# Weight pieces one a block, from one queue, in a sliding-window attention kernel with a two-token expert

## The chip, the cores and the metric

The kernel runs on one core of one Trainium2 chip. The metric is the device time of that core in microseconds; the kernel before takes 795.97 (median of three runs, 795.15 to 799.0). A difference under about half a per cent is not told from no change.

## The reference

One sequence of 2048 tokens, width 640, bf16. Two branches share the normalised input `xn`:

```
xn = layernorm(x)
s  = attention(xn):  q = xn @ wq, 32 heads of width 192;  keys and values are the last 512 rows
                     of the caches;  softmax(q k^T / sqrt(192)) v;  all heads @ wo
B  : r = xn @ w_r;  the 2 tokens with the largest r go through
       y = (silu(x_sel @ w_gate) * (x_sel @ w_up)) @ w_down * sigmoid(r_sel)   (inner width 1536)
     B = xn, with y added at those two rows
out = x + s * silu(B)
```

Nearly all the arithmetic is the attention. The expert touches two rows, but its three weights (640 x 1536, twice, and 1536 x 640) must be loaded whole.

## The kernel before

**Blocks.** The heads are taken in 8 groups of 4. A step is one group's pair of heads for 512 tokens; it has two blocks, each with two score tiles (halves `a` = 0 and 1) of 128 tokens by 2 heads by 512 keys. There are 128 blocks; a round of 16 belongs to one group. The first 12 and the last 2 have an order written out by hand (`FIRST`, `LAST`); blocks 12 to 125 all run

`BLOCK = "A S0 M0 W m E0 B S1 M1 P E1 l"`

- `A`, `B` (`q_phase`, L340): the two halves of the query product for the next step; ScalarE then copies the result out (L352).
- `S0`, `S1` (L367): score products. `M0`, `M1` (L372): row maxima on VectorE. `E0`, `E1` (`exps`, L377): the exponentials on ScalarE, then at once the transpose `pT` of that half by a DMA from SP (L381). The exponentials' buffer `p_ring` has two blocks, so `E0` of block b waits until the transpose of block b - 2 has landed.
- `P` (`o_item` of block b - 2): products with the values (L406), between the two halves whatever stands in `bg[b]`; then scaling on ScalarE and VectorE and the transpose `oT` from SP (L423).
- `W` (`w_item` of block b - 6, L447): product with `wo`, added into `s_acc` by VectorE.
- `m` runs what stands in `mid[b]`, `l` what stands in `end[b]` and `loads[b]`.

**The next group's data.** `group_loads` puts keys, query weights, values and output weights of the next group at fixed blocks of each round, all on SP's queue. GpSimd reorders keys (`k_order`, L121) ahead of their DMA transpose from SP (L125), and copies output weights to the other half of the partitions (`wo_double`, L151).

**The second branch** is spread over blocks 11 to 105 by the lists `bg`, `mid`, `end` and `loads`; nothing else sets its place. All instructions are written in one order and each engine takes its own in that order. Blocks 12 to 28 compute r, 28 to 41 find the two tokens and normalise them into `xsT`. Then:

- `m_ffn_piece(fb, q, eng)` (L751): one of ten pieces (128 partitions x 512, 128 KB) of third `fb` of gate and up, into one buffer `wgu`. That buffer and `wd`, `y4` and `y_bc` are one place in memory: each waits until the one ahead is used up.
- `m_ffn(fb)`: `mul` (products L787, in `bg`; the copy and the tanh), `act` on GpSimd, `turn` (the transpose `hT` from SP, L802).
- `m_wd_piece(h, q)` (L809): one of six pieces (160 KB) of half `h` of the down weight, always from ScalarE. `m_down(h)` (L827): its product. `m_sig` scales the selection masks.
- `m_sum`, `m_own_gate`, `m_change`: the two result rows are summed, gated, and the change in them written to memory and broadcast to all partitions (`y_bc`, 640 KB) from GpSimd's queue.
- `m_gate(n)`: silu of token tile n in place in `xn`: a tanh on ScalarE (L863), two products on GpSimd. `m_add(n)` (L877, L878): adds the two changed rows by mask, on GpSimd.
- `fin_load(n)`: token tile n of x on SP. `fin_pre(n)` (L941, L942): GpSimd multiplies `s_acc` by the gate and adds x. The last group's `w_item` then only adds its own part.

ScalarE's and SP's transfers are issued in each engine's own program order, so whatever a transfer waits for holds up the instructions behind it on that engine.

Of the kernel before, what the change touches and what calls it, by code (L numbers as in the profile page):

```python
# [21 lines left out]
def kernel(ctx, tc, A_x, A_k_cache, A_v_cache, A_wq, A_wo, B_x, B_w_r, B_w_gate, B_w_up, B_w_down, out):  # L22
    nc = tc.nc
# [10 lines left out]
    DC = D // P  # L34
    FC = F // P
# [38 lines left out]
    def f_tile(shape, dtype, name, kind="q"):  # L74
        return banks[kind].tile(shape, dtype, name=name, tag="f")
# [405 lines left out]
    bg = defaultdict(list)  # L481
    mid = defaultdict(list)
    end = defaultdict(list)
    loads = defaultdict(list)
# [260 lines left out]
    def m_ffn_piece(fb, q, eng):  # L745
        def f():
            if q == 0:
                M["wgu"] = M["w"].tile([P, 2, DC, 512], BF16, name="wgu", tag="w")
            w, dc = divmod(q, DC)
            src = (B_w_gate, B_w_up)[w].rearrange("(c p) f -> p c f", p=P)  # L750
            eng.dma_start(out=M["wgu"][:, w, dc, :], in_=src[:, dc, fb * 512:(fb + 1) * 512])  # L751
        return f
# [28 lines left out]
    def m_ffn(fb):  # L781

        def mul():
            gu = f_tile([P, 2, P], FP32, "gu_ps")
            for dc in range(DC):
                for c in range(4):
                    nc.tensor.matmul(gu[32 * c:32 * c + 32], lhsT=M["xsT"][:, dc, :], rhs=M["wgu"][:, :, dc, c * P:(c + 1) * P],  # L787
                                     start=(dc == 0), stop=(dc == DC - 1), skip_group_check=True)
            th = M["s"].tile([P, 3, P], FP32, name="th", tag="t2")
            nc.vector.tensor_copy(out=th[:, 0:2], in_=gu)  # L790
            nc.scalar.activation(out=th[:, 2], in_=th[:, 0], func=ACT.Tanh, scale=0.5)
            M["th"] = th

        def act():
            th = M["th"]
            M["h"] = M["s"].tile([P, P], BF16, name="h")
            nc.gpsimd.tensor_tensor(out=th[:, 2], in0=th[:, 2], in1=th[:, 0], op=ALU.mult)
            nc.gpsimd.tensor_tensor(out=th[:, 2], in0=th[:, 2], in1=th[:, 0], op=ALU.add)
            nc.gpsimd.tensor_tensor(out=M["h"], in0=th[:, 2], in1=th[:, 1], op=ALU.mult)

        def turn():
            nc.sync.dma_start_transpose(out=M["hT"][:, fb * 4:(fb + 1) * 4, :].rearrange("p c t -> p (c t)"), in_=M["h"])  # L802
        return mul, act, turn

    def m_wd_piece(h, q):
        def f():
            if q == 0:
                M["wd"] = M["w"].tile([P, FC, HD], BF16, name="wd", tag="w")
            nc.scalar.dma_start(out=M["wd"][:, 2 * q:2 * q + 2, :],  # L809
                              in_=B_w_down.rearrange("(c p) d -> p c d", p=P)[:, 2 * q:2 * q + 2, h * HD:(h + 1) * HD])  # L810
        return f
# [10 lines left out]
    def m_down(h):  # L822
        def f():
            ys = f_tile([P, HD], FP32, "y_ps")
            for fb in range(FB):
                for c in range(4):
                    nc.tensor.matmul(ys[32 * c:32 * c + 32], lhsT=M["hT"][:, fb * 4 + c, :], rhs=M["wd"][:, fb * 4 + c, :],  # L827
                                     start=(fb == 0), stop=(fb == FB - 1), skip_group_check=True)
            if h == 0:
                M["yp"] = M["s"].tile([P, D], FP32, name="yp", tag="t2")  # L830
                nc.vector.tensor_scalar(out=M["yp"][:, 0:HD], in0=ys, scalar1=M["wrow"][:, 0:1], scalar2=None, op0=ALU.mult)
            else:
                nc.scalar.activation(out=M["yp"][:, HD:D], in_=ys, func=ACT.Copy, scale=M["wrow"][:, 0:1])
        return f
# [32 lines left out]
    def m_gate(n):  # L867
        def f():
            tz = M["s"].tile([P, D], FP32, name="tz", tag="t2")
            gate_of(tz, xn[:, n, :], xn[:, n, :])  # L870
        return f

    def m_add(n):
        def f():
            for j in range(2):
                yh = M["s"].tile([P, D], FP32, name="yh", tag="t2")
                nc.gpsimd.tensor_scalar(out=yh, in0=M["y_bc"][:, j, :], scalar1=M["oh"][:, n, j:j + 1], scalar2=None, op0=ALU.mult)  # L877
                nc.gpsimd.tensor_tensor(out=xn[:, n, :], in0=xn[:, n, :], in1=yh, op=ALU.add)  # L878
        return f
# [16 lines left out]
        if it is not None:  # L896
            spot(29 + b).append(it)
    loads[41].append(m_xsT)
    pieces = {0: (33, (2, 2, 2, 1, 2, 1)), 1: (43, (2, 2, 2, 2, 2)), 2: (49, (2, 2, 2, 1, 2, 1))}
    for fb, km in enumerate((43, 49, 57)):  # L900
        k0, counts = pieces[fb]
        q = 0
        for b, n in enumerate(counts, k0):
            loads[b].append(m_ffn_piece(fb, q, nc.scalar))
            if n == 2:
                mid[b + 1].append(m_ffn_piece(fb, q + 1, nc.sync))
            q += n
        mul, act, turn = m_ffn(fb)
        bg[km].append(mul)
        mid[km + 1].append(act)  # L910
        loads[km + 1].append(turn)
    for h in range(2):
        for q, a in enumerate((57, 58, 58, 59, 59, 60)):
            loads[a + 6 * h].append(m_wd_piece(h, q))
    mid[60].append(m_sig)
    bg[62].append(m_down(0))
    bg[69].append(m_down(1))
    bg[70].append(m_sum)
    for n, b in enumerate((28, 29, 45, 46, 47, 48, 51, 52, 53, 54, 55, 56, 59, 60, 61, 71)):
        bg[b].append(m_gate(n))  # L920
        bg[75 + 2 * n].append(m_add(n))
    bg[27].append(lambda: nc.scalar.preload_act_table_set("exp_and_others"))
    bg[72].append(m_own_gate)
    bg[73].append(m_change)


    def fin_open():
# [5 lines left out]
    def fin_load(n):  # L933
        def f():
            fin_x[n] = fin_pool["x"].tile([P, D], BF16, name="x_fin")
            nc.sync.dma_start(out=fin_x[n], in_=x_v[:, n, :])
        return f

    def fin_pre(n):
        def f():  # L940
            nc.gpsimd.tensor_tensor(out=s_acc[:, n, :], in0=s_acc[:, n, :], in1=xn[:, n, :], op=ALU.mult)  # L941
            nc.gpsimd.tensor_tensor(out=s_acc[:, n, :], in0=s_acc[:, n, :], in1=fin_x[n], op=ALU.add)  # L942
        return f

    bg[106].append(fin_open)
    for n in range(NTB):
        loads[108 + n].append(fin_load(n))
        bg[110 + n].append(fin_pre(n))

    LAG = 6  # L950
    BLOCK = "A S0 M0 W m E0 B S1 M1 P E1 l".split()
# [89 lines left out]
```

## Time and profile before

| | |
|---|---|
| median of the runs | 795.97 us |
| the profiled execution | 797.2 us, of which the span from first to last instruction is 795.3 |
| TensorE clock granted | 0.998 |
| busy: TensorE, VectorE, ScalarE, GpSimd | 776.7, 580.2, 527.6, 338.8 us |
| transfers of gate and up: ScalarE's queue, SP's queue | 17, 13 (128 KB each) |
| transfers of down: ScalarE's queue | 12 (160 KB each) |
| transposes pT, oT on SP's queue by DMA | 246, 126 |

In the profile PE is TensorE, DVE VectorE, ACT ScalarE, POOL GpSimd; a q behind an engine's name is its queue, where transfers are issued and which does no arithmetic. A row of the timeline has start and length in us, the line of the kernel, what is written from what, and how often; in brackets the engine's idle time ahead of it and what seems to have ended that. The chain is followed back from the last instruction: at each step to what let it start. In it a DMA row runs from issue to landing.

### The profile page before, as it was taken

The numbers are of one execution on the slowest core, as the hardware profiler recorded it, in microseconds if no ns is written. First come the engines' busy times: TensorE is split into PE (matmuls) and PEld (weight loads), VectorE is DVE, ScalarE is ACT, GpSimd is POOL, SyncE is SP. The second block draws the span as 40 slices with busy tenths as digits, with TensorE's granted clock in tenths as the row PEclk, the third lists the DMA queues.
The fourth block names the chain that finished last, engine by engine and source line by source line (L and its number), as shares of the span: only waits on it lengthen the run. The fifth ranks groups of instructions, "written<-read, shape, count | busy, mean of one in ns | idle before, by whom it ended". The sixth has DMA issues, their size and how long they took to land.

```text
span 795.3 us, 26980 instructions
## 1 busy us (share of the span) xinstructions
PE 776.7 (98%) x11356; PEld 572.9 (72%) x11356; DVE 580.2 (73%) x1069; ACT 527.6 (66%) x954; POOL 338.8 (43%) x280
## 2 busy tenths in 40 slices
PE   8899999999999998999999999999999999999997
PEld 4457677777777775777677777777777777777775
DVE  7898788887787775767666666767777767766775
ACT  6676666677666675776666766666666666666662
POOL 1333120023210234344311569847954741555875
PEclk9999999999999999999999999999999999999999
DMA  9989999999999999999999999999999999999992
GB/s 236 196 170 173 173 194 161 149 191 166 170 204 189 178 192 181 190 188 206 195 192 184 157 191 190 176 152 184 175 164 185 147 178 187 193 172 175 183 177 85
DMA packets 447130, 142.18 MB, mean 179 GB/s; under 512 B 414180, under 2 KB 446438, under 8 KB 447008
## 3 DMA queue, kind: packets, MB, share of 16 engines
q1 hardware_dynamic: 439184, 132.58, 99.3%
q10 hardware_dynamic: 6800, 5.02, 2.9%
q0 software_dynamic: 1024, 2.85, 1.3%
q8 instruction: 89, 1.46, 0.8%
q14 instruction: 33, 0.27, 0.1%
HBM read 40.31 MB, written 2.63 MB: 54 GB/s over the span
## 4 chain that ended last, share of the span: by engine, by line
PE 87%; DMA 5%; DVE 3%; ACT 3%; issue 1%; SPq 0%; ACTq 0%; DVEq 0%
PE w L447 24%; PE q_ps L340 23%; PE o_ps L406 20%; PE s L367 19%; DMA pT<-pexp 3%; ACT pexp L377 1%; DVE nm L372 1%; PE q_ps L309 1%; DMA oT<-o_sb 1%; DMA v_sb<-in_A_v_cache_dram 1%; DMA wgu<-in_B_w_up_dram 0%; ACT xnT L283 0%; DMA x_in<-in_A_x_dram 0%; PE tp L282 0%; SPq L381 0%
## 5 line engine op out<-in xcount | busy, mean ns | idle before, releaser
L372 DVE TENSOR_REDUCE nm<-s 128x2 f32<-128x1024 f32 x256 | 313.0, 1223 | 137.7 <-PE s L367 135.9
L377 ACT ACTIVATE pexp<-s,nm 128x512 bf16<-128x512 f32 x512 | 324.2, 688 | 98.3 <-DVE nm L372 89.1
L447 PE MATMUL w<-wo_g,oT 64*128 64x320 bf16 x3072 | 231.1, 296 | 1.6 <-DMA oT<-o_sb 1.6
L340 PE MATMUL q_ps<-xnT,wq_g 64*128 64x512 bf16 (+1 forms) x2340 | 232.6, 323 | 0.0
L367 PE MATMUL s<-kT,qT 64*128 64x512 bf16 x1536 | 211.6, 376 | 2.8 <-ACT pexp L377 2.5
L447 PEld LDWEIGHTS <-oT 64*128 64x128 bf16 x3072 | 170.1, 94 | 59.8 <-DMA oT<-o_sb 1.9
L406 PEld LDWEIGHTS <-pT 64*128 64x128 bf16 x4096 | 177.3, 94 | 31.0 <-issue 2.6
L406 PE MATMUL o_ps<-v_sb,pT 64*128 64x193 bf16 x4096 | 195.6, 243 | 2.2 <-DMA pT<-pexp 1.2
L420 ACT ACTIVATE o_sb<-o_ps,rl 128x192 bf16<-128x192 f32 x250 | 91.6, 418 | 131.7 <-DVE rl L413 126.5
L340 PEld LDWEIGHTS <-wq_g 64*128 64x128 bf16 x2340 | 125.8, 99 | 46.0 <-DVE qT L313 0.5
L367 PEld LDWEIGHTS <-qT 64*128 64x128 bf16 x1536 | 84.9, 94 | 57.8 <-issue 3.7
L151 POOL COPY wo_g<-wo_g 64x1920 bf16<-64x1920 bf16 x32 | 57.4, 1796 | 142.5 <-DMA wo_g<-in_A_wo_dram 133.9
L470 DVE TENSOR_TENSOR s_acc<-s_acc,w 128x320 f32<-128x320 f32 x192 | 85.0, 484 | 32.7 <-PE w L447 32.6
L352 ACT ACTIVATE qT<-q_ps 128x1024 bf16<-128x1024 f32 x114 | 92.4, 811 | 8.1 <-PE q_ps L340 2.1
L417 DVE TENSOR_TENSOR o_sb<-o_ps,rl 128x384 bf16<-128x384 f32 x131 | 73.0, 557 | 4.5
L121 POOL COPY k_perm<-k_raw 128x768 bf16<-128x768 bf16 x30 | 24.3, 824 | 104.7 <-DMA k_raw<-in_A_k_cache_dram 68.0
L877 POOL TENSOR_SCALAR yh<-y_bc,oh 128x640 f32<-128x640 f32 x32 | 60.2, 1882 | 6.1 <-DMA y_bc<-y_d 3.3
L864 POOL TENSOR_TENSOR tz<-tz,xn 128x640 f32<-128x640 f32 x16 | 22.4, 1398 | 65.2 <-ACT tz L863 65.2
L878 POOL TENSOR_TENSOR xn<-xn,yh 128x640 bf16<-128x640 bf16 x32 | 45.0, 1405 | 2.7
L413 DVE RECIPROCAL rl<-o_ps 128x2 f32<-128x2 f32 x256 | 30.6, 160 | 12.2 <-PE o_ps L406 7.7
L942 POOL TENSOR_TENSOR s_acc<-s_acc,x_fin 128x640 f32<-128x640 f32 x16 | 22.4, 1398 | 34.7 <-DMA x_fin<-in_A_x_dram 30.1
L478 POOL TENSOR_TENSOR fin_o<-fin_t,s_acc 128x640 bf16<-128x640 f32 x12 | 18.5, 1542 | 14.1 <-DVE fin_t L473 14.0
(138 smaller groups left out, 279.3 us busy)
## 6 DMA issues: line engine op xcount, KB each, us to landing
wo_g<-in_A_wo_dram SPq DMA_DIRECT2D x32, 240.0 KB, 4.1
k_raw<-in_A_k_cache_dram SPq DMA_DIRECT2D x32, 192.0 KB, 3.6
v_sb<-in_A_v_cache_dram SPq DMA_DIRECT2D x32, 192.0 KB, 4.3
wq_g<-in_A_wq_dram SPq DMA_DIRECT2D x14, 288.0 KB, 3.7
pT<-pexp SPq DMA_TRANSPOSE x246, 4.1
wq_g<-in_A_wq_dram SPq DMA_DIRECT2D x14, 192.0 KB, 3.9
x_fin<-in_A_x_dram SPq DMA_DIRECT2D x16, 160.0 KB, 3.5
oT<-o_sb SPq DMA_TRANSPOSE x126, 3.6
```

Of the source, the lines that this page charges most:

```text
L151: nc.gpsimd.tensor_copy(out=grp[g][("wo", pr)][half(1), cs, :], in_=grp[g][("wo", pr)][half(0), cs, :])
L340: mm = nc.tensor.matmul(q_ps[k][:, 0:n] if type(q_ps) is list else q_ps[:, k, 0:n], lhsT=wq[half(r), dc, c:2 * Dh:3], rhs=xnT[half(r), tok ...
L352: nc.scalar.activation(out=out, in_=q_ps[:, :, 0:n], func=ACT.Copy, scale=scale)
L367: nc.tensor.matmul(s_of[b, a][:, r, :], lhsT=qT_of[i][half(r), c, u * P:(u + 1) * P], rhs=grp[g][("kT", pr)][half(r), :, c, :], start=(c = ...
L372: rm = nc.vector.tensor_reduce(out=nm_of[b, a], in_=s_of[b, a], axis=AX.X, op=ALU.max, negate=True)
L377: nc.scalar.activation(out=p_ring[:, b % 2, a, :, hh, :].rearrange("p (x j) e -> p x j e", x=2), in_=s_of[b, a][:, hh, :].rearrange("p (j ...
L406: nc.tensor.matmul(o_of[b][r][:, a, 0:Dh + 1], lhsT=pT_ring[half(r), b % RP, a, k, :], rhs=v_ring[half(r), (g * PAIRS + pr) % RV, k, 0:Dh ...
L417: nc.vector.tensor_tensor(out=o_sb, in0=src, in1=rl[:, r].unsqueeze(2).unsqueeze(3).to_broadcast([P, 2, 3, HK]), op=ALU.mult)
L420: nc.scalar.activation(out=o_sb[:, a], in_=src[:, a], func=ACT.Copy, scale=rl[:, r, a:a + 1])
L447: nc.tensor.matmul(w_ps[r][:, 0:HD], lhsT=oT_ring[half(r), bs[pr] % RT, c, :], rhs=grp[g][("wo", pr)][half(r), c, cs], start=(pr == 0 and ...
L470: nc.vector.tensor_tensor(out=acc, in0=acc, in1=src, op=ALU.add)
L877: nc.gpsimd.tensor_scalar(out=yh, in0=M["y_bc"][:, j, :], scalar1=M["oh"][:, n, j:j + 1], scalar2=None, op0=ALU.mult)
```

## The change

All of it is in the lists of the second branch; no instruction is added or removed.

- Gate and up pieces: one a block, all from ScalarE, in blocks 32 to 41, 43 to 52 and 54 to 63. Before they were one or two a block in 33 to 38, 43 to 47 and 49 to 54; of two, the second was issued by SP in the next block's `m`, ahead of that block's transposes. That is 13 pieces that leave SP.
- Their products: 43, 54, 65 (before 43, 49, 57), with `act` and `turn` one block later as before.
- Down pieces: one a block in 65 to 70 and 72 to 77 (before 57 to 60 and 63 to 66, one or two a block). Their products: 72 and 79 (before 62, 69); the sum 80 (70); `m_own_gate` and `m_change` 82 and 83 (72, 73).
- Gates: 28, 29, 45 to 53, 56 to 60 (before 28, 29, 45 to 48, 51 to 56, 59 to 61, 71).
- Adds: sixteen from block 85 to 109, five in eight blocks (before every second block from 75 to 105).
- Last preparation: x loads from block 112 to 124, preparations 114 to 126, five in four blocks (before one a block from 108 and 110); the second branch's memory is given up in block 111 (before 106).

```diff
-    pieces = {0: (33, (2, 2, 2, 1, 2, 1)), 1: (43, (2, 2, 2, 2, 2)), 2: (49, (2, 2, 2, 1, 2, 1))}
-    for fb, km in enumerate((43, 49, 57)):
-        k0, counts = pieces[fb]
-        q = 0
-        for b, n in enumerate(counts, k0):
-            loads[b].append(m_ffn_piece(fb, q, nc.scalar))
-            if n == 2:
-                mid[b + 1].append(m_ffn_piece(fb, q + 1, nc.sync))
-            q += n
+
+    for fb, km in enumerate((43, 54, 65)):
+        for q in range(2 * DC):
+            loads[(32, 43, 54)[fb] + q].append(m_ffn_piece(fb, q, nc.scalar))
         mul, act, turn = m_ffn(fb)
         bg[km].append(mul)
         mid[km + 1].append(act)
         loads[km + 1].append(turn)
     for h in range(2):
-        for q, a in enumerate((57, 58, 58, 59, 59, 60)):
-            loads[a + 6 * h].append(m_wd_piece(h, q))
+        for q in range(FC // 2):
+            loads[65 + 7 * h + q].append(m_wd_piece(h, q))
     mid[60].append(m_sig)
-    bg[62].append(m_down(0))
-    bg[69].append(m_down(1))
-    bg[70].append(m_sum)
-    for n, b in enumerate((28, 29, 45, 46, 47, 48, 51, 52, 53, 54, 55, 56, 59, 60, 61, 71)):
+    bg[72].append(m_down(0))
+    bg[79].append(m_down(1))
+    bg[80].append(m_sum)
+    for n, b in enumerate((28, 29, *range(45, 54), *range(56, 61))):
         bg[b].append(m_gate(n))
-        bg[75 + 2 * n].append(m_add(n))
+        bg[85 + 8 * n // 5].append(m_add(n))
...
-    bg[72].append(m_own_gate)
-    bg[73].append(m_change)
+    bg[82].append(m_own_gate)
+    bg[83].append(m_change)
...
-    bg[106].append(fin_open)
+    bg[111].append(fin_open)
     for n in range(NTB):
-        loads[108 + n].append(fin_load(n))
-        bg[110 + n].append(fin_pre(n))
+        loads[112 + 4 * n // 5].append(fin_load(n))
+        bg[114 + 4 * n // 5].append(fin_pre(n))
```

## The prediction

> **What bounds the kernel now.** I read the page first (busy shares), then the chain that ended last in order of time, then the stretches where that chain leaves TensorE, and there the waits and the timeline of SP and ACT.
>
> ```profile
> PE 776.7 (98%) x11356; PEld 572.9 (72%) x11356; DVE 580.2 (73%) x1069; ACT 527.6 (66%) x954; POOL 338.8 (43%) x280
> ```
>
> TensorE is busy 98% of 795.3 us, so only its gaps can be won. The chain has one row for the output product of nearly every block (start, length, what):
>
> ```profile
> 269.11 1.64 PE w L447 x24
> 275.77 1.63 PE w L447 x24
> ...
> 287.55 1.63 PE w L447 x24
> 295.48 5.84 DMA pT<-pexp
> 315.84 1.63 PE w L447 x24
> ...
> 369.60 1.64 PE w L447 x24
> ...
> 395.87 1.63 PE w L447 x24
> ...
> 461.37 1.63 PE w L447 x24
> 470.50 6.98 DMA pT<-pexp
> 479.56 1.64 PE w L447 x24
> ...
> 750.39 1.64 PE w L447 x24
> ```
>
> From 479.56 to 750.39 lie 46 blocks, 5.888 us each: the pace at which nothing is missing. 269.11 to 275.77 is block 43 with the first gate and up product, 6.66, so a product costs 0.77, and I take a down product at the same. These five stay. Three places are longer than their products explain:
> - 287.55 to 315.84, blocks 46 to 49: 28.29 for four blocks and a product, 28.29 - 23.55 - 0.77 = 3.97 lost.
> - 369.60 to 395.87, blocks 59 to 62: 26.27 for four blocks and a down product, 26.27 - 23.55 - 0.77 = 1.95 lost.
> - 461.37 to 479.56, blocks 74 to 76: 18.19 for three blocks, 18.19 - 17.66 = 0.53 lost.
>
> Together 6.45 us, all between blocks 46 and 76, where the change works. The timeline of the first place shows SP and ACT:
>
> ```profile
> 280.01 0.37 SPq L751 DMA_DIRECT2D wgu<-in_B_w_gate_dram  x1
> ...
> 287.38 0.56 SPq L751 DMA_DIRECT2D wgu<-in_B_w_gate_dram  x1
> ...
> 288.91 1.27 ACT L377 ACTIVATE pexp<-s,nm 128x512 bf16<-128x512 f32 x2 [0.96 <-DVE nm L372]
> ...
> 294.78 0.59 SPq L751 DMA_DIRECT2D wgu<-in_B_w_up_dram  x1
> ...
> 294.80 1.27 ACT L377 ACTIVATE pexp<-s,nm 128x512 bf16<-128x512 f32 x2 [0.42 <-DVE nm L372]
> ...
> 295.48 1.27 SPq L381 DMA_TRANSPOSE pT<-pexp  x1
> ...
> 298.46 1.27 ACT L377 ACTIVATE pexp<-s,nm 128x512 bf16<-128x512 f32 x2
> ...
> 301.35 0.35 ACTq L751 DMA_DIRECT2D wgu<-in_B_w_up_dram  x1
> ...
> 301.75 1.27 ACT L377 ACTIVATE pexp<-s,nm 128x512 bf16<-128x512 f32 x2 [2.02 <-DVE s_acc L470]
> ...
> 302.46 0.89 SPq L751 DMA_DIRECT2D wgu<-in_B_w_up_dram  x1
> ...
> 303.46 1.24 SPq L381 DMA_TRANSPOSE pT<-pexp  x1
> ...
> 308.81 1.27 ACT L377 ACTIVATE pexp<-s,nm 128x512 bf16<-128x512 f32 x2 [2.48 <-DMA pT<-pexp]
> ...
> 309.65 0.60 SPq L751 DMA_DIRECT2D wgu<-in_B_w_up_dram  x1
> ...
> 313.04 0.29 PE L787 MATMUL gu_ps<-wgu,xsT 128*32 128x256 bf16 x4 [1.81 <-DMA wgu<-in_B_w_up_dram]
> ```
>
> SP is the late one. Block 46's first exponentials end at 288.91 + 1.27 = 290.18, and their transpose is issued at 295.48, 5.3 us later; block 47's end at 296.07 and are issued at 303.46, 7.4 later. Three things follow. ACT's own weight load stands from 299.73 (298.46 + 1.27) to 301.35: in the built program the transfers of SP and ACT take eight completion counters in turn, a transfer waits until the one eight issues before has landed, and this one's predecessor is the transpose of 295.48, which lands at 295.48 + 5.84 = 301.32 by the chain. The exponentials of block 49 start at 308.81, when block 47's transpose has left their buffer; at the block's pace they were due at 294.80 + 2 x 5.888 = 306.58. And the last weight piece, issued by the late SP at 309.65, keeps the product waiting for another 1.81 at 313.04.
>
> **The change, part by part.** *Gate and up pieces.* Thirty pieces stay; the 13 that SP issued go to ACT, and they are one a block in 32 to 41, 43 to 52, 54 to 63 where there had been up to two. Four of SP's stand ahead of block 47's first transpose: 0.37 + 0.56 + 0.59 + 0.89 = 2.41, and 0.11 between two rows (294.78 + 0.59 to 295.48), 0.44: 2.85 us. It then lands at 308.81 - 2.85 = 305.96, ahead of the 306.58 at which it is needed. The margin is only 0.6 by issue time; with one 128 KB piece less in flight each block it grows, by an amount that no row isolates. The last piece of each product comes two blocks ahead of it, so the 1.81 goes too. I take all 3.97. On ACT 13 more issues at 0.34 are 4.4 us over 30 blocks:
>
> ```profile
> 293.62 0.34 ACTq L751 DMA_DIRECT2D wgu<-in_B_w_up_dram  x1
> ...
> 293.67 0.70 ACT L377 ACTIVATE pexp<-s,nm 128x512 bf16<-128x512 f32 x1
> ```
>
> The exponential runs beside the issue, so a plain issue costs nothing; a held one costs what it is held beyond ACT's spare time (2.02 against its usual 0.96 above). Of before's 29 weight loads on ACT 21 have a counter whose last transfer is of the previous or the same block, of the 42 now only 9, the others two blocks back: ACT is held less.
>
> *Down pieces* go from six in four blocks (57 to 60, again 63 to 66) to one a block in 65 to 70 and 72 to 77, and the third product and its transpose hT from 57/58 to 65/66. In the second place:
>
> ```profile
> 375.51 1.20 SPq L802 DMA_TRANSPOSE hT<-h  x1
> ...
> 376.82 6.37 DMA pT<-pexp
> ...
> 383.22 0.38 ACTq L809 DMA_DIRECT2D wd<-in_B_w_down_dram  x1
> ```
>
> (The middle row is the chain's: issue and time to landing.) hT is issued ahead of the transpose of 376.82, and two down loads a block go on beside it; it lands at 383.19, and at 383.22 ACT's next load is let go, whose counter it holds. In the changed kernel those blocks have one gate or up piece of 128 KB for two down pieces of 160, and no hT: 1.20 us sooner at the least. I take the 1.95. What was there meets blocks 65 to 67 instead, with half the loads a block. Its price is between 0 and the same 1.95; I take 0.3, near the low end, because the queue arrives less late.
>
> *The broadcast of the two changed rows* (y_bc, 640 KB, broadcast by POOL) goes from block 74/75 to 84/85. The lost 0.53 is a transpose that took 6.98 beside it. Blocks 100 and 101 stand where 84 and 85 stand in the round of 16 blocks, and there SP has idle time (617.77 + 1.24 to 620.67):
>
> ```profile
> 617.77 1.24 SPq L381 DMA_TRANSPOSE pT<-pexp  x1
> ...
> 620.67 1.21 SPq L423 DMA_TRANSPOSE oT<-o_sb  x1
> ```
>
> I take 0.5. *The adds and the last preparation* are POOL's: 16 adds of 2 x (1.88 + 1.41) = 6.6 us in 25 blocks instead of 31, 105 of 147 us; preparations of 2.8 us in 13 blocks instead of 16, ending one block later.
>
> ```profile
> L877 POOL TENSOR_SCALAR yh<-y_bc,oh 128x640 f32<-128x640 f32 x32 | 60.2, 1882 | 6.1 <-DMA y_bc<-y_d 3.3
> ...
> L878 POOL TENSOR_TENSOR xn<-xn,yh 128x640 bf16<-128x640 bf16 x32 | 45.0, 1405 | 2.7
> ...
> 770.75 1.40 POOL L942 TENSOR_TENSOR s_acc<-s_acc,x_fin 128x640 f32<-128x640 f32 x1
> ...
> 773.56 1.55 POOL L478 TENSOR_TENSOR fin_o<-fin_t,s_acc 128x640 bf16<-128x640 f32 x1 [1.42 <-DVE fin_t L473]
> ...
> 781.47 1.53 POOL L478 TENSOR_TENSOR fin_o<-fin_t,s_acc 128x640 bf16<-128x640 f32 x1 [3.07 <-DVE fin_t L473]
> ```
>
> POOL idles 1.42 + 3.07 = 4.5 us behind the last preparation, which covers one more of 2.8 us: nothing; without that cover it would be 2.8 at the end. SP waits for POOL at the k transposes, three or four blocks after their copies: nothing. It waits at the last x loads too, whose buffer the preparation of the same block or the one before frees. SP comes to such a load at the block's end or later; where that is too early it waits up to 2.8 us, which a transpose that is not late already can bear: nothing. The gates keep their number and come one a block at most; ACT and POOL, 66% and 43% busy, hide them: nothing.
>
> Sum: 3.97 + 1.95 + 0.5 - 0.3 = 6.1 us. The profiled execution took 797.2 around its span of 795.3 and would take 791.1; it stands 1.2 above the median of the runs, 795.97, from which 6.1 leads to 789.9. That is my forecast, with its own range 789.5 (all 6.45 won) to 791.5 (the 1.95 all back at blocks 65 to 67).
>
> **The rivals.** *The traffic is the limit, not SP's issuing.* The 16 DMA engines look full everywhere (share 1.06 and 1.07 below, where 1 is all engines busy), so pieces that change queues may delay the transposes as before. Against it, by stretches (span, PE busy, the other engines, clock, DMA share, GB/s):
>
> ```profile
> 268.00:327.00 59.00, 55.64 (x844) 40.52 (x840) 38.77 (x68) 39.33 (x73) 20.64 (x18) 1.00 1.07 185
> 598.00:692.00 94.00, 94.00 (x1409) 71.21 (x1406) 65.87 (x113) 62.40 (x113) 46.31 (x31) 1.00 1.06 176
> ```
>
> The stretch that loses moves 185 GB/s and the one that loses nothing 176, at the same DMA share; a share that does not tell them apart proves no limit. If it is one, halving the pieces a block halves the losses: 6.45 / 2 = 3.2, so 792.8. The Trainium skill, DMA: Bandwidth & Descriptors, Issuing engines are not separate DMA queues, speaks for this rival: transfers started by different engines run on the same 16 DMA engines, and a second issuer only saves sequencer time, usually small beside the transfer. By that rule the move to ACT alone would gain nothing, and the trace disagrees in so far as SP's issue time is itself what is short here.
>
> *ACT is held by its own loads.* 42 instead of 29 stand in front of its exponentials. Two of 29 were let go only by a landing in the rows above (301.35 and 383.22). If one of the 13 more is held so long that a place like the first comes of it, 3.97 goes back: 789.9 + 4.0 = 793.9.
>
> *Slower: SP never catches up.* One load a block from 32 to 77 leaves no gap for recovery. If a transpose is more than 5 us late at each peak of the round (blocks 47 to 49, 63 to 67, 79 to 81), each costs the 3.97 of the first place: 795.97 - 6.45 + 3 x 3.97 = 801.4. The mechanism decides from the point where a transpose lands after the exponentials two blocks on. SP's 13 issues fewer and the idle time above speak against it.
>
> **How the numbers follow.** 0.5% is 4.0 us, about what a measurement can tell from no change: faster is below 792.0, slower above 799.9. Forecast 0.71; traffic 0.14 and ACT held 0.06, both inside 0.5%; slower 0.09. So 0.71, 0.20, 0.09. The range 788.0 to 794.5 takes in the likeliest case and both middle ones; its low end lies 1.5 under 789.5, since the runs shown differ by more than that among themselves (795.15 to 799.0). It leaves out the slower case and the tails.
>
> **What would show it.** Right: the chain's output products at 5.89 from block 44 on except about 0.8 more at 43, 54, 65, 72 and 79; no exponential waiting for pT; no product waiting for wgu; block 47's first transpose under 5 us late. Wrong: a gap at 47 to 49 or 63 to 67 with SP late (traffic), ACT's weight loads starting over 1 us after its last exponential (held), or POOL's last work behind DVE's. The forecast fails if the losses come back at the new places or if the runs without a profiler do not lose the 6.45.

## The result and the profile after

| | before | after |
|---|---|---|
| median of 17 runs each, taken beside one another | 795.97 us | 792.75 us |
| lowest to highest of them | 793.09 to 799.11 | 791.66 to 794.59 |
| the profiled execution (span) | 797.2 (795.3) | 793.03 (791.3) |

The ratio is 0.996, 95% interval 0.9946 to 0.9974. The changed kernel is 3.2 us faster, 0.4%. The forecast was 789.9 (6.1 won), range 788.0 to 794.5. The gain has the right sign and half the size, and lies inside the 0.5% that the prediction took as no change; that it is told from no change at all is due to the many runs. The time is inside the stated range because that range took in two of the rivals as well. The range that the forecast gave itself, 789.5 to 791.5, ends below it, and none of the 28 runs of the changed kernel (these 17 and 11 later ones) is under 790.91. The ends of the spread say more than the medians: the lowest runs lie 1.4 us apart, the highest 4.5.

The busy row of the changed kernel's page, within 1.5 us of before's for every engine:

```profile
PE 777.6 (98%) x11356; PEld 571.5 (72%) x11356; DVE 579.0 (73%) x1069; ACT 527.9 (67%) x954; POOL 338.8 (43%) x280
```

Its chain in order of time (start, length, what), the output product of a block or what stands in its place:

```profile
204.53 1.63 PE w L447 x24
212.40 4.83 DMA oT<-o_sb
222.51 1.64 PE w L447 x24
...
263.74 1.63 PE w L447 x24
269.79 3.54 DMA xsT<-xsel
276.60 1.63 PE w L447 x24
...
300.16 1.63 PE w L447 x24
307.16 5.61 DMA oT<-o_sb
318.06 1.64 PE w L447 x24
...
348.28 1.63 PE w L447 x24
356.31 4.59 DMA oT<-o_sb
366.19 1.65 PE w L447 x24
...
401.52 1.64 PE w L447 x24
408.18 1.63 PE w L447 x24
...
450.16 1.63 PE w L447 x24
...
485.48 1.64 PE w L447 x24
```

The three places of before are whole: 276.60 to 300.16 is blocks 44 to 47, four at 5.89 (23.56); 366.19 to 401.52 is six at 5.89; 450.16 to 485.48, blocks 73 to 78, six at 5.89. In place of the lost 6.45 stand four small gaps: 204.53 to 222.51 is three blocks and 0.32 (blocks 33 and 34), 263.74 to 276.60 two blocks, a product and 0.31 (43), 300.16 to 318.06 three blocks and 0.24 (50), 348.28 to 366.19 three blocks and 0.25 (58). In the chain each has a late transpose from SP, xsT or oT. Together they make 1.1. From 401.52 to 408.18 is the block with the third product, 6.66: nothing beside it is lost at 65 to 67.

SP and ScalarE around block 47 in the changed kernel, from the timeline:

```profile
295.63 1.27 ACT L377 ACTIVATE pexp<-s,nm 128x512 bf16<-128x512 f32 x2 [0.43 <-DVE nm L372]
...
300.88 1.45 SPq L381 DMA_TRANSPOSE pT<-pexp  x1
...
307.40 1.27 ACT L377 ACTIVATE pexp<-s,nm 128x512 bf16<-128x512 f32 x2 [0.43 <-DVE nm L372]
```

Block 47's first exponentials end at 295.63 + 1.27 = 296.90, their transpose is issued at 300.88, 4.0 us late (7.4 before). The exponentials of block 49, at 307.40, wait for VectorE, not for the transpose. One wait for a transpose stands elsewhere, in block 65:

```profile
402.99 1.27 ACT L377 ACTIVATE pexp<-s,nm 128x512 bf16<-128x512 f32 x2 [0.53 <-DMA pT<-pexp]
```

Block 63's first transpose was issued 5.0 us late and block 64's 5.5, the latest of blocks 32 to 80. TensorE loses nothing by it: 401.52 to 408.18 is a block and its product.

The end has become longer. The timeline of SP and of the value products in the last blocks:

```profile
759.55 1.74 SPq L931 DMA_DIRECT2D x_fin<-in_A_x_dram  x1
...
764.62 5.07 SPq L381 DMA_TRANSPOSE pT<-pexp  x3
...
769.79 0.84 PE L406 MATMUL o_ps<-v_sb,pT 64*128 64x193 bf16 x16 [0.61 <-DMA pT<-pexp]
```

The last x load stands in block 124 and holds SP for 1.74 us; the transposes behind it are late, and a value product waits 0.61. From block 124's first score product to the end the changed kernel takes 40.88 us, the kernel before 39.88.

So the two profiled executions differ by 797.2 - 793.0 = 4.2 us: 6.45 of stalls gone, 1.1 of new ones, 1.0 more at the end and 0.2 before block 14 (97.47 for 97.28) leave 4.15.

### The profile page after: what moved, and what is told of

Same layout as the page of the kernel before. It is cut to its first block, busy times and chain, and to the rows that moved or that the text cites. A ratio compares the mean times of both kernels' runs of the same rounds, so it can differ in the third digit from the quotient of the medians.

```text
span 791.3 us, 26980 instructions
## 1 busy us (share of the span) xinstructions
PE 777.6 (98%) x11356; PEld 571.5 (72%) x11356; DVE 579.0 (73%) x1069; ACT 527.9 (67%) x954; POOL 338.8 (43%) x280
## 3 DMA queue, kind: packets, MB, share of 16 engines
q8 instruction: 89, 1.46, 0.8%
## 4 chain that ended last, share of the span: by engine, by line
PE 89%; DMA 4%; DVE 3%; ACT 2%; issue 1%; SPq 0%; DVEq 0%; ACTq 0%
PE w L447 24%; PE q_ps L340 23%; PE o_ps L406 20%; PE s L367 19%; DMA oT<-o_sb 2%; DVE nm L372 2%; ACT pexp L377 1%; PE q_ps L309 1%; DMA x_in<-in_A_x_dram 1%; DMA pT<-pexp 1%; DMA v_sb<-in_A_v_cache_dram 1%; DMA xsT<-xsel 0%; DVE fin_o L475 0%; PE tp L282 0%; PE gu_ps L787 0%
## 5 line engine op out<-in xcount | busy, mean ns | idle before, releaser
L865 POOL TENSOR_TENSOR xn<-tz,xn 128x640 bf16<-128x640 f32 x16 | 22.4, 1398 | 1.3
```

## The experiments

The theory at the start was the prediction's: SP has too little time to issue, so every issue taken off it helps. The rivals were the traffic of all transfers, and ScalarE held by its own loads. The kernel before ran beside each group of kernels; its medians there were 794.27 (35 runs, 791.66 to 799.07) for the first four kernels, 794.97 (24 runs, 792.25 to 799.32) for the next four and 795.06 (23 runs, 792.1 to 797.73) for the last four.

**Only the queue.** In the kernel before, ScalarE issues SP's 13 pieces at the same places.

```diff
-                mid[b + 1].append(m_ffn_piece(fb, q + 1, nc.sync))
+                mid[b + 1].append(m_ffn_piece(fb, q + 1, nc.scalar))
```

> The kernel before with one thing changed: the 13 pieces that SP issued are issued by ACT at the same places, so up to two a block stay. If SP's issue time is what was short, the transposes come up to 2.8 us sooner at block 47 and most of the change's 3.2 us is won: about 793. If the traffic is what was short, nothing changes: 796. If ACT's loads hold ACT (two a block now stand on its queue, each behind a transfer eight issues before), it is slower than before: 798 or more.

Measured 793.23 (791.49 to 797.25), ratio 0.9983, interval 0.9963 to 1.0004: about 1 us, and not told from none. Its profiled execution still loses 1.5 us beside the product in blocks 47 to 49 and 0.7 in 52 and 53. The move alone is not the whole. The rows of the second of these places say where the rest goes (the first row is the chain's, from issue to landing):

```profile
322.24 5.63 DMA pT<-pexp
...
326.95 0.33 ACTq L751 DMA_DIRECT2D wgu<-in_B_w_gate_dram  x1
327.89 0.34 ACTq L751 DMA_DIRECT2D wgu<-in_B_w_up_dram  x1
328.33 1.27 ACT L377 ACTIVATE pexp<-s,nm 128x512 bf16<-128x512 f32 x2 [2.50 <-DVE s_acc L470]
...
330.56 0.73 PE L340 MATMUL q_ps<-xnT,wq_g 64*128 64x256 bf16 x10 [0.45 <-ACT qT L352]
```

The transpose of 322.24 lands at 327.87, and at 327.89 ScalarE's second load, eight issues behind it, is let go; the first had waited in the same way for an output transpose that landed at 326.93. The exponentials behind them had their row maxima at 326.76 and their buffer before that. So the loads hold them for 1.6 us, and TensorE then waits 0.45 for the copy that follows them. In block 48 the issues of two loads add 1.35 us to a transpose that lands late itself, and TensorE waits 0.91. By the completion counters that the trace records, 34 of the 42 weight loads on ScalarE have a counter whose last transfer is of the previous block in this kernel, and 9 of 42 in the changed one, as the prediction counted. So the rival in which ScalarE is held by its own loads does happen when the queue alone is changed.

**Only the spreading.** In the changed kernel SP issues every second piece.

```diff
-            loads[(32, 43, 54)[fb] + q].append(m_ffn_piece(fb, q, nc.scalar))
+            loads[(32, 43, 54)[fb] + q].append(m_ffn_piece(fb, q, (nc.scalar, nc.sync)[q % 2]))
```

> The changed kernel with every second gate and up piece issued by SP (15 of 30), still one a block. If SP's issue time is what was short, most of the gain goes back: 795 to 796. If the number of pieces a block (traffic) is what was short, nothing goes back: 792.7.

Measured 794.38 (792.98 to 796.48), ratio 1.0003, interval 0.9988 to 1.0019: spreading alone shows no gain, as the theory had it. SP issues 15 pieces here, two more than in the kernel before, and the longer end stays. The closer comparison is with the changed kernel, which differs in the queue of these 15 pieces alone: its ratio is 0.9960 (0.9969 when it was taken again, below), and neither interval reaches this one. The 15 pieces, 9.6 us of issues on SP, cost 0.34 to 0.43% or 2.7 to 3.4 us, by way of the kernel before. In the profiled execution, the fastest of the 12 runs, 1.3 us of that stand at block 65, where the product waits for a piece that SP issued. Against the kernel before, neither part alone shows a gain that its interval clears; both together do.

**Only the late end.** The kernel before with the sum, the broadcast, the adds, the x loads and the preparations of the changed one; one gate goes from block 71 to 58.

```diff
-    bg[70].append(m_sum)
+    bg[80].append(m_sum)
...
-        bg[75 + 2 * n].append(m_add(n))
+        bg[85 + 8 * n // 5].append(m_add(n))
...
-    bg[72].append(m_own_gate)
-    bg[73].append(m_change)
+    bg[82].append(m_own_gate)
+    bg[83].append(m_change)
...
-    bg[106].append(fin_open)
+    bg[111].append(fin_open)
...
-        loads[108 + n].append(fin_load(n))
-        bg[110 + n].append(fin_pre(n))
+        loads[112 + 4 * n // 5].append(fin_load(n))
+        bg[114 + 4 * n // 5].append(fin_pre(n))
```

> The kernel before with only the second half of the change: the sum at block 80, the broadcast of the two rows at 83, adds from 85 to 109, x loads 112 to 124, preparations 114 to 126; one gate moves from 71 to 58 to make that possible. My prediction gave this half 0.5 us of gain (the 0.53 beside the broadcast) and nothing for the end: 795.5. The trace after shows 0.8 us lost in block 125, behind the last x loads: with it 796.3.

Measured 793.49 (791.79 to 796.55), ratio 0.9989, interval 0.9971 to 1.0006. At the median neither size can be told. The profile bears out both: no gap at 76, and 40.91 us from block 124 to the end, where the kernel before has 39.88. It held a surprise: with the weights as in the kernel before, this execution lost 0.9 us at block 49 and 0.4 at 62 beside the products, not 3.97 and 1.95.

**Only the weights.** The changed kernel with the x loads and preparations as before; the adds are drawn together into blocks 85 to 105, and the broadcast stays late.

```diff
-        bg[85 + 8 * n // 5].append(m_add(n))
+        bg[85 + 4 * n // 3].append(m_add(n))
...
-    bg[111].append(fin_open)
+    bg[106].append(fin_open)
...
-        loads[112 + 4 * n // 5].append(fin_load(n))
-        bg[114 + 4 * n // 5].append(fin_pre(n))
+        loads[108 + n].append(fin_load(n))
+        bg[110 + n].append(fin_pre(n))
```

> The changed kernel with the last preparation back where it was before (x loads from block 108, preparations from 110), and the adds in blocks 85 to 105 to make room. If the 0.8 us of block 125 belong to the moved preparation, this takes 0.8 less than the changed kernel, 791.9; if they are chance, 792.7. More adds a block on POOL (6.6 us every 7.85) could also delay the key copies: then over 793.

Measured 792.18 (791.09 to 794.47), ratio 0.9983, interval 0.9967 to 0.9999; from block 124 to the end 40.07. The long end belongs to the late x loads. Its weights come as in the changed kernel, and yet its profiled execution lost 0.66 us at block 49 and 0.65 at 58, and issued block 47's first transpose 5.4 us late.

**The changed kernel again, and with its end one block earlier.** These two ran side by side; the edit of the second:

```diff
-    bg[111].append(fin_open)
+    bg[110].append(fin_open)
...
-        loads[112 + 4 * n // 5].append(fin_load(n))
-        bg[114 + 4 * n // 5].append(fin_pre(n))
+        loads[111 + 4 * n // 5].append(fin_load(n))
+        bg[113 + 4 * n // 5].append(fin_pre(n))
```

> The changed kernel once more, beside the other runs of this job. Theory (the stalls of blocks 46 to 76 vary from execution to execution, the changed kernel loses none of them): 1.5 to 3 us below the kernel before at the median (ratio about 0.997), its highest run at least 3 us below the highest of before, its lowest within 1 us of the lowest of before; the profile again without a gap over 0.4 us beside the products in blocks 44 to 76, and with its end 0.8 to 1.0 us longer than that of before. Rival (the first comparison was luck of the runs): ratio 0.999 to 1.001, and a spread as wide as that of before.

> The changed kernel with the x loads and the last preparations one block earlier (memory given up in 110, loads from 111 to 123, preparations from 113 to 125). Theory (the last x load, in block 124, holds SP for 1.7 us and makes block 125's values product wait for its transpose): the end from block 124 on is back to 39.9 to 40.1 us, 0.8 below the changed kernel's, and the median 0.8 below it. Rival (the end is longer because POOL or the traffic is later as a whole): the end keeps 40.8 to 40.9, the median that of the changed kernel.

The changed kernel took 792.15 (790.91 to 793.46), ratio 0.9969, interval 0.9954 to 0.9985: 2.8 us, near the 3.2 of the first comparison. Its gap at 58 was 0.50, a little over what was expected, its end 40.71. One block earlier took 792.25 (791.23 to 792.8), ratio 0.9971, interval 0.9955 to 0.9988; its end is 40.29. That is just above the 39.88 to 40.27 of the six profiled executions with the x loads as before, so in the profile most of the lost time at the end comes back; at the median nothing that could be told. The forecast of 0.8 there was missed.

**Twice the bytes at the same issues.** In the changed kernel each piece loads two slices.

```diff
-            eng.dma_start(out=M["wgu"][:, w, dc, :], in_=src[:, dc, fb * 512:(fb + 1) * 512])
+            ds = slice(min(dc, DC - 2), min(dc, DC - 2) + 2)
+            eng.dma_start(out=M["wgu"][:, w, ds, :], in_=src[:, ds, fb * 512:(fb + 1) * 512])
```

> The changed kernel with every gate and up piece loading two slices instead of one, 256 KB for 128 (the slice beside it again, which is overwritten with the same values): as many issues at the same places on the same queue, 3.9 MB more traffic in blocks 32 to 63. Theory (the issuing engine's time is what was short, not the 16 DMA engines): the same as the changed kernel within 0.6 us, no gap over 1 us in blocks 44 to 65. Rival (the traffic is the limit): the transposes land later by the added bytes, 3.9 MB over some 180 GB/s is 21 us of all engines in 31 blocks, or 0.7 a block, so that SP and the transposes fall behind over several blocks: gaps in blocks 38 to 65 again, at least 3 us in sum, 795 or more where the changed kernel has 792.

Measured 797.34 (796.31 to 798.49), ratio 1.004, interval 1.0022 to 1.0057: 5.2 us over the changed kernel beside it. The theory, that issuing alone counts, fell here. SP issues none of these bytes, and yet its transposes are late. What TensorE waited for in this run:

```profile
PE o_ps L406 <- DMA pT<-pexp: 3.6, 5, 1.4
...
PE w L447 <- DMA oT<-o_sb: 0.8, 1, 0.8
```

(us in total, times, the longest.) In the changed kernel the first of these is 1.8 in 2:

```profile
PE o_ps L406 <- DMA pT<-pexp: 1.8, 2, 1.2
```

In the changed kernel TensorE waits for no wgu; before that cost 1.81.

**Twice the issues at the same bytes, on SP.** In the kernel before, each of SP's 13 pieces goes in two transfers of 64 partitions.

```diff
-            eng.dma_start(out=M["wgu"][:, w, dc, :], in_=src[:, dc, fb * 512:(fb + 1) * 512])
+            for ps in ((slice(0, P),), (slice(0, P // 2), slice(P // 2, P)))[eng is nc.sync]:
+                eng.dma_start(out=M["wgu"][ps, w, dc, :], in_=src[ps, dc, fb * 512:(fb + 1) * 512])
```

> The kernel before with each of SP's 13 gate and up pieces cut into two transfers of 64 partitions: the same bytes at the same places, 13 issues more on SP. Theory (SP's issue time is what is short): an issue more at 0.4 to 0.6 us each, four of them ahead of block 47's first transpose, which is then some 2 us later; the losses at blocks 46 to 49 grow by as much, the median by 1 to 2.5 us, ratio 1.002 to 1.003. Rival (the traffic is the limit, or a transfer's issue is short for half the rows): within 0.4 us of the kernel before.

Measured 801.0 (799.19 to 805.7), ratio 1.0102, interval 1.0076 to 1.0128: 6.0 us lost, more than twice what was expected. The timeline of its first place:

```profile
294.51 1.26 ACT L377 ACTIVATE pexp<-s,nm 128x512 bf16<-128x512 f32 x2 [0.43 <-DVE nm L372]
294.79 1.24 SPq L752 DMA_DIRECT2D wgu<-in_B_w_up_dram  x2
...
302.79 1.59 SPq L752 DMA_DIRECT2D wgu<-in_B_w_up_dram  x2
304.48 1.25 SPq L381 DMA_TRANSPOSE pT<-pexp  x1
...
309.43 1.26 ACT L377 ACTIVATE pexp<-s,nm 128x512 bf16<-128x512 f32 x2 [3.01 <-DMA pT<-pexp]
...
313.75 0.41 PE L788 MATMUL gu_ps<-wgu,xsT 128*32 128x256 bf16 x4 [1.75 <-DMA wgu<-in_B_w_up_dram]
```

A pair of halves holds SP 1.24 to 1.59 us. Block 47's first transpose is issued at 304.48, 8.7 us after 294.51 + 1.26; the exponentials of block 49 wait 3.01 for it, the product another 1.75 for its last piece. It is the chain of events that the prediction read in the kernel before, each part a little longer. All rows of wgu on SP together are 16.4 us here and 6.9 in the kernel before: 9.5 us more on SP cost 6.0.

**Twice the issues on ScalarE.** All 30 pieces of the changed kernel in two transfers.

```diff
-            eng.dma_start(out=M["wgu"][:, w, dc, :], in_=src[:, dc, fb * 512:(fb + 1) * 512])
+            for ps in (slice(0, P // 2), slice(P // 2, P)):
+                eng.dma_start(out=M["wgu"][ps, w, dc, :], in_=src[ps, dc, fb * 512:(fb + 1) * 512])
```

> The changed kernel with all 30 gate and up pieces cut into two transfers of 64 partitions on ScalarE's queue: the same bytes, 30 issues more on ScalarE and none on SP. Theory (SP's issuing time is scarce, ScalarE's is not): 30 times 0.34 us beside 34% idle time, so within 0.6 us of the changed kernel, 792 to 792.8. Rival (an issue costs the same on whichever engine): 13 more on SP cost 6 us, 0.46 each, so 30 cost 13.8 us, 806; or ScalarE is held by its own loads, 4 us, 796.

Measured 792.16 (791.35 to 795.37), ratio 0.9972, interval 0.9955 to 0.9988: the changed kernel's own ratio was 0.9969. Thirty issues more on ScalarE in the changed kernel cost nothing that can be told at the median, thirteen on SP in the kernel before cost 6 us. Its runs spread wider, though: five of the 12 took 793.7 to 795.4, where the changed kernel's 11 beside the kernel before end at 793.46.

**Half the bytes at the same issues.** The pieces of the kernel before load 256 of 512 columns, and the products read that half twice; the expert's arithmetic on the other half is left out.

```diff
-            eng.dma_start(out=M["wgu"][:, w, dc, :], in_=src[:, dc, fb * 512:(fb + 1) * 512])
+            eng.dma_start(out=M["wgu"][:, w, dc, 0:256], in_=src[:, dc, fb * 512:fb * 512 + 256])
...
-  rhs=M["wgu"][:, :, dc, c * P:(c + 1) * P]
+  rhs=M["wgu"][:, :, dc, c % 2 * P:c % 2 * P + P]
```

> The kernel before with each gate and up piece loading 256 of its 512 columns (64 KB), the same issues at the same places on the same queues; the products read the loaded half twice, so the expert's arithmetic on the other half is left out. Theory (SP's issuing decides, and the traffic weighs in by what it adds to each issue and landing): half the added traffic of twice the bytes, taken off. That was 5.2 us for 3.9 MB, so up to 2.6 us for the 2 MB here if it goes down as it went up, to 792.4 where the kernel before has 795; less if SP's 13 issues alone make SP late, and block 47's first transpose is still over 6 us late. Rival (the issues count and the bytes do not): within 0.5 us of the kernel before, block 47's first transpose over 7 us late.

Measured 793.48 (791.21 to 795.94), ratio 0.9974, interval 0.9958 to 0.9989: 1.6 us at the medians. The bytes weigh in the kernel before too. They are not all: the profiled execution, the highest of these runs at 795.94, issued block 47's first transpose 6.2 us late and lost 4.3 us beside the product in block 49.

How long the transposes of blocks 32 to 64 take to land, by the view of the transfers (number, median us from issue to landing), from the fewest bytes to the most. Half the bytes, in the kernel before, which has 4.4 and 3.7 with all of them:

```profile
pT<-pexp SPq DMA_TRANSPOSE x67, 4.0
...
oT<-o_sb SPq DMA_TRANSPOSE x33, 3.2
```

The changed kernel:

```profile
pT<-pexp SPq DMA_TRANSPOSE x67, 4.5
...
oT<-o_sb SPq DMA_TRANSPOSE x33, 4.3
```

Twice the bytes:

```profile
pT<-pexp SPq DMA_TRANSPOSE x66, 4.5
...
oT<-o_sb SPq DMA_TRANSPOSE x33, 4.7
```

In the twelve profiled executions at the usual bytes, whatever the kernel, pT takes 3.9 to 4.5 and oT 3.4 to 4.4. So oT lies outside that spread on both sides, as if its landing moved with the bytes; pT does not show it.

**Fewer issues on SP still: the output weights from ScalarE.** On the kernel with the end one block earlier.

```diff
-            at(b, lambda c=c: wo_piece(g, c, nc.sync))
+            at(b, lambda c=c: wo_piece(g, c, nc.scalar))
```

> The changed kernel with its end one block earlier, and the four output weight loads of each later group issued by ScalarE instead of SP, at the same places: four issues of 0.6 us off SP in each round of 16 blocks. Theory (what is left beside the products, 0.35 us at block 50, 0.28 in the first blocks and 0.3 at the end, is SP's lateness at the top of each round): the latest transpose of blocks 32 to 80 under 3.8 us, 0.3 to 0.8 us below the changed kernel, 791.5. Rival (ScalarE is held by loads that wait for their buffer): 0.5 to 3 us above it.

Measured 792.15 (791.91 to 792.42, 6 runs), ratio 0.9954, interval 0.9937 to 0.9971. SP is less late in the mean (1.2 us for 2.0 with the end one block earlier, blocks 32 to 63), but its latest transpose of blocks 32 to 80 is not: 4.2 us in both, where under 3.8 was expected. The gaps did not go either: 0.96 at block 49 and 0.25 at 40. The median is the changed kernel's. It does not beat it by anything that these runs can tell; what is left beside the products is not SP's lateness alone.

**The kernel before, another execution.**

> The kernel before, another profiled execution. Theory (its stalls vary from execution to execution, and the first profiled one lost more than most): the losses of blocks 46 to 49, 59 to 62 and 74 to 76 are between 1 and 6 us in sum, the same for the products, and block 47's first transpose is again over 5 us late. Rival (the 6.45 us stand in every execution, and what was gained by the change there is lost elsewhere): 6.2 to 6.7 us in sum again.

It took 791.56, in one run, and lost under 1 us at the three places together. Its chain at them:

```profile
287.56 1.63 PE w L447 x24
...
299.33 1.63 PE w L447 x24
305.65 4.14 DMA wgu<-in_B_w_up_dram
312.63 1.63 PE w L447 x24
...
366.39 1.64 PE w L447 x24
...
390.70 1.63 PE w L447 x24
```

299.33 to 312.63 is two blocks, a product and 0.75; 366.39 to 390.70, blocks 59 to 62, is 24.31, four blocks and a product (23.55 + 0.76), nothing lost. The timeline says where it parts from the first profiled execution of the same program:

```profile
288.92 1.26 ACT L377 ACTIVATE pexp<-s,nm 128x512 bf16<-128x512 f32 x2 [0.96 <-DVE nm L372]
...
293.41 1.27 SPq L381 DMA_TRANSPOSE pT<-pexp  x1
...
294.81 1.27 ACT L377 ACTIVATE pexp<-s,nm 128x512 bf16<-128x512 f32 x2 [0.43 <-DVE nm L372]
...
300.99 1.24 SPq L381 DMA_TRANSPOSE pT<-pexp  x1
...
309.84 0.29 PE L787 MATMUL gu_ps<-wgu,xsT 128*32 128x256 bf16 x4 [0.57 <-DMA wgu<-in_B_w_up_dram]
```

The exponentials of blocks 46 and 47 start within 0.01 us of where the prediction's rows have them (288.91, 294.80). The transposes behind them are issued at 293.41 and 300.99, where it had 295.48 and 303.46. Of the first place's 3.97 us 3.2 go with SP being 2 us later in one execution than in the other, while what it serves stands at the same times. Where SP falls behind can be read from two rows of the first execution and the same two of this one:

```profile
272.80 1.86 SPq L136 DMA_DIRECT2D v_sb<-in_A_v_cache_dram  x1
...
288.05 2.68 SPq L381 DMA_TRANSPOSE pT<-pexp  x1
```

```profile
272.54 0.59 SPq L136 DMA_DIRECT2D v_sb<-in_A_v_cache_dram  x1
...
286.68 1.25 SPq L381 DMA_TRANSPOSE pT<-pexp  x1
```

In the first execution the one transfer took 1.27 us longer to issue and the other 1.43. Behind the two, SP is 2.80 us later there than here, and 2.07 after a longer issue in the present one.

## Why the prediction was right or wrong

**Right: where and by what.** The three places were whole in both profiled executions of the changed kernel. Block 47's first transpose is 4.0 us late there and 4.6 in the second (forecast: under 5), and no product waits for wgu. These signs tell less than they seem to: the second execution of the kernel before has 4.9, and the kernel with only the weights, 5.4. One exponential does wait for pT, 0.5 us in block 65 in both, at no cost to TensorE. That an issue on SP is dearer than one on ScalarE holds: 15 pieces cost 2.7 to 3.4 us on SP in the changed kernel, and 13 issues more on SP cost 6.0 in the kernel before, while 30 more on ScalarE in the changed kernel cost nothing at the median. The rival in which ScalarE is held by its loads is out for the changed kernel, but thanks to the spreading: with the queue alone ScalarE was held. The slower rival is out too: neither profiled execution lost more than 0.5 us in a block beside its product. Its price, 3.97 us wherever a transpose is over 5 us late, was too high: at blocks 63 and 64 two are, and nothing is lost. The output products stand at 5.89 except at 43, 54, 65, 72 and 79 and at the four small gaps.

**Wrong: "from which 6.1 leads to 789.9".** The prediction summed 6.45 us of stalls in an execution of 797.2 and took the sum off the median. They are not a constant of the program: another execution of it loses 0.75 at the same places and takes 791.56, and over 99 runs in four comparisons it takes 791.66 to 799.32. The two executions differ by 5.64 us in time and by 5.70 in these stalls. The 1.2 us by which the profiled execution stood above the median were part of those stalls, and the step took them off twice. From 797.2 the sum gives 791.1, and with 1.0 at the end, 0.8 more of new losses (1.1 for 0.3) and 0.2 before block 14 it comes to 793.1; the profiled execution took 793.0. The median of before has less to lose: 795.97 - 792.75 = 3.2. That 792.75 lies in the stated range is luck as far as this step goes: the range was wide enough for the rivals, and the step's error, 2.9 us, is nearly as large as the gain. The prediction named this case: it would fail "if the runs without a profiler do not lose the 6.45".

**Wrong: "a transpose that is not late already can bear: nothing".** The last x loads cost 1.0 at the end in the first profiled execution. The step looked at POOL's cover, which held (it still waits 2.09 us for VectorE behind the last preparation), and at a load's wait of some blocks; it didn't ask in which block the last load now stands. In 124 the next transposes are of the last blocks, with no later block to catch up in. The kernel with only the late end has the same 40.9; the one with the end as before has 40.1.

**Wrong in size and place: "I take 0.3" for new losses at 65 to 67.** Those blocks lose nothing. 1.1 came at 33 and 34, 43, 50 and 58 instead (0.6 and 0.35 by the same count in the second profiled execution and in the one with an earlier end).

**Half right: the traffic as a rival.** Its 792.8 is nearly the median. That is not its proof, since the losses were not halved: in the profile they went. But "a share that does not tell them apart proves no limit" left out that traffic need not fill the engines to matter. Its bytes cost 5.2 us when doubled on ScalarE's queue, and halving them in the kernel before won 1.6. The two causes meet in SP, as I read it. Its issuing in blocks 32 to 63, worked out from all its rows (a long issue is over 0.5 us longer than the median of its kind):

| kernel, profiled execution | SP issues | long ones | transposes, mean us | SP's time a block | mean lateness of pT |
|---|---|---|---|---|---|
| before, 797.2 | 149 | 23 | 1.45 | 5.65 | 2.9 |
| before, 791.56 | 150 | 17 | 1.42 | 5.51 | 1.9 |
| before, only the queue, 794.05 | 136 | 26 | 1.49 | 5.50 | 2.0 |
| before, half the bytes, 795.94 | 149 | 18 | 1.40 | 5.44 | 1.9 |
| before, halves on SP, 799.19 | 162 | 19 | 1.41 | 5.77 | 3.0 |
| after, 793.03 | 133 | 18 | 1.46 | 5.27 | 2.3 |
| after, every second piece on SP, 792.98 | 147 | 17 | 1.39 | 5.34 | 2.5 |
| after, twice the bytes, 797.19 | 133 | 24 | 1.53 | 5.49 | 2.9 |
| after, end one block earlier, output weights on ScalarE, 792.42 | 127 | 17 | 1.43 | 5.09 | 1.2 |

Without losses these blocks take 5.98 us in the mean in the kernel before, with their four products, and 5.94 in the changed one, with two. More issues fill SP. At 5.3 to 5.8 us of work a block it catches up slowly, and the lateness is a matter of how the execution falls out. That is my reading of the table; the runs show each of the two prices, not how they add. SP's time alone does not order the kernels: half the bytes (793.48 at the median) and twice the bytes (797.34) stand next to each other, and the last kernel, whose SP has the most time left, is no faster than the changed one. That more bytes make a transpose's issue longer is not shown either. The issue of pT and oT is 1.25 to 1.27 us in the median of each of these executions, and the means differ by how many take over 1.75: 19 of 95 with twice the bytes, but also 20 of 96 with only the queue changed. With twice the bytes TensorE waits directly for landings that come late.

The Trainium skill's rule that the prediction set against its theory (DMA: Bandwidth & Descriptors, Issuing engines are not separate DMA queues) fits the runs as it stands: the transfers of ScalarE's queue do delay those of SP, as the doubled bytes show, and a piece's issue on SP is short beside its transfer (0.53 us in the mean of the kernel before, where landing takes 3.4 to 3.7). That the move would gain nothing, as the prediction drew from it, does not follow on an engine as full as SP: there 13 issues more cost 6.0 us.

**Open.** The first execution's SP is 2 us later than the second's because single issues took up to 1.4 us longer; why they did the rows do not say. The trace shows why the queue alone falls short (ScalarE is then held too), but its ratio, 0.9983 with an interval up to 1.0004, does not say by how much.

## What to carry to other kernels

Before a sum of stalls from one profile is taken off a median, look at the spread of the runs: where the fastest run is already near the time without the stalls, only the mean loss can be won, and the distance from the median is not to be taken off again. Count the issuing engine as a resource of its own (its issues times their length against the length of a block): near full, an issue taken off it is worth a part of its own length (here 9.5 us of issues more cost 6.0 in the kernel before, and 9.6 cost about 3 in the changed one), if the engine that takes it over is not itself held by what the issue waits for; bytes on another queue can still make its transfers land later. When work is moved towards the end, ask which block holds its last transfer and whether any block is left to absorb it.

## What the runs showed of the hardware

In two executions of one program, both at a granted clock of 0.998, ScalarE's exponentials of blocks 46 and 47 started within 0.01 us of each other, and yet one took 797.2 us and the other 791.56: SP's queue had taken different times to issue the same transfers (1.86 us for 0.59, 2.68 for 1.25). Whether both ran on one chip is not on record; the 35 runs of the first group, on record for one chip, spread from 791.66 to 799.07. An issue is not of fixed length: that of the transposes pT and oT took 1.25 to 1.27 us in the median of blocks 32 to 63 of every kernel here, and over 1.75 in 10 to 20 of some 96. And the same 128 KB piece cost SP 0.37 to 1.02 us to issue in these two executions (0.53 and 0.54 in the mean), ScalarE 0.33 to 0.39.
